# Four PSUM tiles in place of one during the first block of a fused attention and feed-forward kernel

## The chip, the cores and the metric

One Trainium2 chip, one of its cores. The time is the device time of one execution in microseconds (us). Lower is better. TensorE is called PE here, VectorE DVE, ScalarE ACT, GpSimd POOL, and SP is the engine that issues most of the loads and stores.

## What is computed

Three stages follow each other on 2304 rows (4 batches of 576 positions, 512 columns): windowed attention, a gated feed-forward part, and a gated convolution part.

```python
# attention: 8 heads of 64, each position sees itself and 63 before it
scores = scale * q @ k.T                      # masked outside 0 <= i-j < 64
attn = softmax(scores); x = attn @ v          # then heads side by side: (B, 576, 512)
# feed-forward with a mix of each row and the row before it
xk = mu_k*x + (1-mu_k)*x_prev; xr = mu_r*x + (1-mu_r)*x_prev
k = relu(xk @ w_k); v = (k*k) @ w_v; r = sigmoid(xr @ w_r); y = r*v
# five-tap convolution gate
gate = sigmoid(sum_k conv_w[k] * y[t-4+k]); out = (gate * (y @ w_val)) @ w_out
```

## The kernel before

The 2304 rows are cut into five blocks: block 0 has 256 rows, blocks 1 to 4 have 512 each. A **unit** is one block and one pair of heads, so units 0 to 3 are block 0, units 4 to 7 are block 1. For every unit the attention runs through the same steps, and the plan gives each a name:

- `ldqk`, `ldv`: the loads of q, k and v, issued by SP.
- `qk`: the scores, on PE. Units 0 to 3 write them to tiles of the pool `p0` (line 458 to 465), units 4 and up to the first two banks of the shared tile `sv` (line 511).
- `mask` (units 4 and up, DVE, line 518) reads the scores from `sv` and writes the masked ones to SBUF; `edge` on POOL finishes the mask.
- `top`, `exp`, `eps`, `rec`, `norm`: the softmax, on DVE, ACT (line 424), POOL or DVE, and DVE.
- `tp` (units 0 to 3, PE, line 477): transposes of the softmax into the third bank of `sv`; `pt` copies them to SBUF (ACT line 481 or DVE line 482). Later units use a transpose on DVE (`tr`, line 533).
- `pv` (PE, line 488 for units 0 to 3, line 545 later): the values, into the fourth bank of `sv` (all four banks for later units). `x` copies the result to `xT` (ACT line 442 or DVE line 441).

The rest of a block then runs on `xT`: `a` and `xm` mix rows (lines 579 and 592), `r`, `h` and `v` are the three products (line 655 in block 0, line 632 in blocks 1 to 4). PE meets the product `r` first. The weights arrive in pieces: the load `ld`, then `g`, `t`, `s` (lines 348, 351, 353) which convert the words, then `hi` and `lo` (lines 369 to 372) which split each weight in two.

PSUM has eight banks here: `p0` takes four in the first block (two tiles of two banks), `sv` the other four. The pool `pg` takes over the four of `p0` after the last `exp` of block 0 and serves the products.

Nothing is scheduled at run time. Every step is given to a `Plan`, and the table `SLOT` holds a number for each step, by which all of them are sorted; that order is each engine's program order, and a letter (a, v, p) in front of a number says which engine does a step that can run on several. The waits between engines come from the tiles: an instruction that writes a tile waits for the earlier readers of that tile. The four banks of `sv` are one tile, allocated once:

```python
def first_idle():
    Q["sv"] = pq.tile([P, 4, TB], F32, tag="sv", name="sv")
```

`Plan.run` also calls `fill` where its own table of costs sees a gap on PE: it emits matmuls of zeros (line 1197), into `sv` before `pg` exists and into a spare tile of `pg` afterwards, until the first product `r` is emitted.

Of the kernel before, what the change touches and what calls it, by code (L numbers as in the profile page):

```python
# [20 lines left out]
P = 128  # L21
W = 64
# [149 lines left out]
}  # L172

class Plan:

# [1078 lines left out]
```

## Time and profile before

| | us |
|---|---|
| median of three runs | 417.67 (417.37 to 419.25) |
| the profiled execution, its own time | 418.32 |
| span of the profiled execution, first to last instruction | 416.5 |
| PE busy | 405.7 (97% of the span) |
| DVE busy | 341.9 (82%) |
| ACT busy | 256.2 (62%) |
| POOL busy | 28.4 (7%) |

The time of an execution is about 1.8 us longer than its span, which is what lies before the first and after the last instruction. A busy share is an average over stages with different limits: what a change is worth is read in its own stage, from what an engine waited for there. In the rows below, "[1.13 <-DVE s L518]" behind an instruction says that its engine was idle for 1.13 us ahead of it and that the instruction at line 518 on DVE ended the wait. PEclk is the granted clock of PE, 1.00 for 2.4 GHz and 0.50 for 1.2 GHz; a value between says that both levels fell into the stretch.

### The profile page before, as it was taken

The numbers are of one execution on the slowest core, as the hardware profiler recorded it, in microseconds if no ns is written. First come the engines' busy times: TensorE is split into PE (matmuls) and PEld (weight loads), VectorE is DVE, ScalarE is ACT, GpSimd is POOL, SyncE is SP. The second block draws the span as 40 slices with busy tenths as digits, with TensorE's granted clock in tenths as the row PEclk, the third lists the DMA queues.
The fourth block names the chain that finished last, engine by engine and source line by source line (L and its number), as shares of the span: only waits on it lengthen the run. The fifth ranks groups of instructions, "written<-read, shape, count | busy, mean of one in ns | idle before, by whom it ended". The sixth has DMA issues, their size and how long they took to land.

```text
span 416.5 us, 10815 instructions
## 1 busy us (share of the span) xinstructions
PE 405.7 (97%) x4554; PEld 343.0 (82%) x4556; DVE 341.9 (82%) x502; ACT 256.2 (62%) x580; POOL 28.4 (7%) x83
## 2 busy tenths in 40 slices
PE   8599999999999999999999999999999999999996
PEld 4468888878778878777888888888888999999995
DVE  4689899888857848897989898978697899999850
ACT  4769998659553276769424855267631375796741
POOL 3101000001000001000000000000000001023110
PEclk9679999999999999999999999999999999999999
DMA  8976961233113342225443544678999925939945
GB/s 297 412 306 227 330 228 41 68 106 114 59 41 118 137 128 69 82 78 186 134 156 123 211 144 187 214 272 286 347 385 409 368 92 147 248 78 205 218 122 151
DMA packets 26017, 78.36 MB, mean 188 GB/s; under 512 B 2672, under 2 KB 3440, under 8 KB 23920
## 3 DMA queue, kind: packets, MB, share of 16 engines
q1 hardware_dynamic: 23952, 72.64, 48.9%
q0 software_dynamic: 1872, 5.01, 7.2%
q8 instruction: 36, 0.59, 0.6%
q14 instruction: 13, 0.11, 0.1%
q10 hardware_dynamic: 144, 0.00, 0.0%
HBM read 51.80 MB, written 23.49 MB: 181 GB/s over the span
## 4 chain that ended last, share of the span: by engine, by line
PE 95%; ACT 3%; DVE 1%; issue 0%; POOL 0%; DVEq 0%; ACTq 0%; POOLq 0%
PE h L632 21%; PE v L632 21%; PE r L632 11%; PE sv L545 4%; PE h L655 4%; PE v L655 4%; PE sv L511 4%; PE out L1011 3%; PE val1m L901 3%; PE val0m L901 3%; PE val2m L901 3%; PE out2m L901 3%; PE val3m L901 3%; PE out0m L901 3%; PE out1m L901 3%; PE sv L1197 1%
## 5 line engine op out<-in xcount | busy, mean ns | idle before, releaser
L632 PE MATMUL h<-x,wk 128*128 128x512 f32 x384 | 90.5, 393 | 0.0
L632 PEld LDWEIGHTS h<-x,wk 128*128 128x128 f32 x384 | 71.4, 188 | 15.5
L632 PE MATMUL v<-sh,wv 128*128 128x512 f32 x256 | 81.6, 393 | 0.0
L632 PEld LDWEIGHTS v<-sh,wv 128*128 128x128 f32 x256 | 48.0, 188 | 10.8
L424 ACT ACTIVATE s<-s,m 128x96 f32<-128x96 f32 x128 | 46.1, 363 | 12.3 <-DVE m L413 12.2
L632 PE MATMUL v<-sl,wv 128*128 128x512 f32 x128 | 49.9, 390 | 0.0
L632 PE MATMUL r<-x,wr 128*128 128x512 f32 x192 | 45.6, 393 | 0.0
L832 DVE SCALAR_TENSOR_TENSOR early<-early,wc 128x576 f32<-128x576 f32 x48 | 38.4, 813 | 4.7 <-ACT early L830 4.3
L632 PEld LDWEIGHTS r<-x,wr 128*128 128x128 f32 x192 | 35.6, 188 | 7.8
L632 PEld LDWEIGHTS v<-sl,wv 128*128 128x128 f32 x128 | 24.0, 188 | 4.8
L682 ACT ACTIVATE rk<-h 128x512 f32<-128x512 f32 (+1 forms) x27 | 14.2, 536 | 16.7 <-PE h L632 10.8
L424 ACT ACTIVATION_READ_ACCUMULATOR s<-s,m 128x1 f32 x128 | 24.2, 189 | 0.0
L545 PEld LDWEIGHTS sv<-pt,vt 32*64 32x64 f32 x1536 | 18.8, 130 | 5.6 <-issue 2.8
L518 DVE SCALAR_TENSOR_TENSOR s<-sv,band 128x768 f32<-128x768 f32 x16 | 15.3, 955 | 9.2 <-PE sv L511 5.7
L592 DVE SCALAR_TENSOR_TENSOR xm<-xT,omu,xm 128x512 f32<-128x512 f32 x32 | 22.5, 743 | 0.0
L579 ACT ACTIVATE xm<-xT,sm 128x512 f32<-128x512 f32 x26 | 17.0, 712 | 8.0 <-DVE x L615 7.9
L712 DVE TENSOR_TENSOR sl<-rk,sh 128x1024 fp32r<-128x1024 f32 x16 | 19.4, 1220 | 1.5 <-ACT rk L710 1.4
L545 PE MATMUL sv<-pt,vt 32*64 32x32 f32 (+2 forms) x1536 | 20.5, 238 | 0.0
L615 DVE TENSOR_TENSOR x<-xm,x 128x1024 fp32r<-128x1024 f32 x16 | 19.5, 1217 | 0.4 <-ACT x L612 0.4
L511 PEld LDWEIGHTS sv<-qk 64*32 64x32 f32 x1024 | 12.9, 108 | 8.2 <-issue 3.8
L706 ACT ACTIVATE sh<-rk 128x1024 fp32r<-128x1024 f32 x16 | 16.9, 1056 | 3.8 <-DVE rk L684 3.6
L511 PE MATMUL sv<-qk 64*32 64x96 f32 x1024 | 16.5, 255 | 2.7 <-ACT pt L481 1.7
(189 smaller groups left out, 797.4 us busy)
## 6 DMA issues: line engine op xcount, KB each, us to landing
qk<-qk SPq DMA_DIRECT2D x16, 544.0 KB, 4.8
vt<-vh SPq DMA_DIRECT2D x16, 384.0 KB, 3.9
xb<-x2d SPq DMA_DIRECT2D x4, 1152.0 KB, 8.3
out_t<-st SPq DMA_DIRECT2D x15, 288.0 KB, 3.7
x2d<-sgs SPq DMA_DIRECT2D x16, 256.0 KB, 4.0
w_out<-w SPq DMA_DIRECT2D x8, 512.0 KB, 3.0
w_val<-w SPq DMA_DIRECT2D x8, 448.0 KB, 4.2
wk<-w_val SPq DMA_DIRECT2D x2, 1792.0 KB, 11.8
```

The lines of the kernel that those rows point to most:

```text
L424: ACT.activation(out=s, in_=s if t else scores()[:, c // 2, c % 2, :], func=AF.Exp, scale=1.0 if t else D ** -0.5, bias=l(0)[:, c:c + 1], ...
L511: PE.matmul(a["ps"][rows(c), h, j * P:j * P + KW], lhsT=a["q"][heads[h], c * HW:(c + 1) * HW], rhs=a["k"][heads[h], c * HW:c * HW + KW], s ...
L545: PE.matmul(a["o"][heads[h], i, j0 * HW:j1 * HW], lhsT=a["v"][r, k, heads[h]], rhs=p, start=k == 0, stop=k == m + 1, skip_group_check=True)
L579: ACT.activation(out=m[:, i, :n], in_=xT[:, f, 1:1 + n], func=AF.Copy, scale=sm[:, c:c + 1])
L592: V.scalar_tensor_tensor(out=m, in0=xT[:, f, :n], scalar=omu[:, c:c + 1], in1=m, op0=ALU.mult, op1=ALU.add)
L615: lambda E: E.tensor_tensor(out=dst(1), in0=src(), in1=f32(dst(0)), op=ALU.subtract))
L632: PE.matmul(ps, lhsT=a, rhs=b[:, kt, :], start=(kt == 0 and i == 0), stop=(kt == nk - 1 and i == 2))
L655: PE.matmul(Ps[key][:, :n], lhsT=ws(kt), rhs=x()[:, kt, :], start=kt == 0, stop=kt == nk - 1)
L706: ACT.activation(out=Ss[t][0][:, f, :n], in_=rk(), func=AF.Square)
L712: lambda E: E.tensor_tensor(out=Ss[t][1][:, f, :n], in0=rk(), in1=f32(Ss[t][0][:, f, :n]), op=ALU.subtract))
L832: V.scalar_tensor_tensor(out=o, in0=x, scalar=c, in1=o, op0=ALU.mult, op1=ALU.add)
L901: PE.matmul(z[bank][:, j, :HS], lhsT=lhs, rhs=rhs, start=new and kt == 0 and e == 0, stop=kt == 1 and e == 2, skip_group_check=not new)
```

## The change

During the first block the four banks of `sv` are three tiles: `s4` (two banks) for the scores of units 4 and 5, `tp` for the transposes, `pv` for the values. When the values of units 0 to 3 have been copied out and the scores of units 4 and 5 have been masked, the pool is closed and one tile `sv` of four banks takes its place for the rest of the kernel. Matmuls of zeros ahead of `pg` go to the first bank of `s4` until unit 4 has its scores, then to `pv` if `tp` holds something that was not yet read, else to `tp`, and to none if both hold something.

```diff
-    pq = pas.enter_context(tc.tile_pool(name="pq", bufs=1, space=PSUM, side="right"))
+    pzs = ExitStack()
+    pz = pzs.enter_context(tc.tile_pool(name="pz", bufs=1, space=PSUM, side="right"))
...
         def tp():
+            held.add("tp")
...
-                PE.transpose(Q["sv"][:, 2, i * P:(i + 1) * P], a["s"][:, i, :], ident)
+                PE.transpose(Q["tp"][:, i * P:(i + 1) * P], a["s"][:, i, :], ident)
...
         def pv():
-            a["o"] = Q["sv"]
+            held.add("pv")
+            a["o"] = Q["pv"]
...
+        early_scores = u < HP + 2
...
-            a["ps"] = Q["sv"]
+            a["ps"] = Q["s4"] if early_scores else Q["sv"]
...
     def first_idle():
-        Q["sv"] = pq.tile([P, 4, TB], F32, tag="sv", name="sv")
+        Q["s4"] = pz.tile([P, 2, TB], F32, tag="s4", name="s4")
+        Q["tp"], Q["pv"] = (pz.tile([P, TB], F32, tag=n, name=n) for n in ("tp", "pv"))
     op("idle", "none", 0, ["warm"], first_idle)
+
+    def strips_space():
+        pzs.close()
+        Q["sv"] = pas.enter_context(tc.tile_pool(name="pq", bufs=1, space=PSUM, side="right")).tile([P, 4, TB], F32, tag="sv", name="sv")
+    op("sv", "none", 0, [*[("x", u) for u in range(HP)], *[("mask", HP + i) for i in range(2)]], strips_space)
...
-        elif any("ps" in A[u] for u in range(HP, len(UNITS))):
+        elif "ps" not in A[HP]:
+            ps = Q["s4"][:, 0]
+        elif len(held) < 2:
+            ps = Q["pv" if "tp" in held else "tp"]
+        else:
             return
-        else:
-            ps = Q["sv"][:, 0]
```

The table `SLOT` is new from one end to the other, so the order on every engine is another, over the whole kernel. Two of its lines:

```diff
-    'qk': '9 11 19 34 38 57 109 142 177 246 261 304 341 367 387 431 467 497 519 546',
+    'qk': '9 12 19 34 26 57 99 145 180 242 262 312 341 362 398 416 444 493 521 555',
-    'pt': 'a33 a51 v70 a87',
+    'pt': 'a36 a59 a71 a86',
```

Steps that may run on ACT or DVE change sides as well. In all, DVE gains 15 of them (six splits `xhi`, two squares `sq`, two splits of `w_out`, two `ghi`, one `xhi_`, one `ghi_`, one split of `w_k`) and gives up two (`pt` of unit 2 and one split of `w_val`) and two small `eps`. The counts of products and of attention matmuls stay; the matmuls of zeros grow from 24 to 28.

**PE, from the scores of unit 3 on.** Before; `qk_227` and `qk_262` are the inputs of units 4 and 5, `pt` the transposed softmax, `spare` the tile in `pg`:

```order
L465 MATMUL qk_245<-early 64x128 x8
L511 MATMUL sv<-qk_227 32x96 x32
L488 MATMUL sv<-pt_238,sgs 64x64 x8
L477 MATMUL sv<-ident,xm 128x128 x4
L511 MATMUL sv<-qk_262 32x96 x32
L488 MATMUL sv<-pt_316,sgs 64x64 x8
L1197 MATMUL spare<-sgs 128x512
```

Scores, values and transposes alternate, and all of them write `sv`.

The same place in the changed kernel, from the scores of unit 2 on (`qk_190` and `qk_295` are the inputs of units 4 and 5, `s_122` is the tile `s4`):

```order
L467 MATMUL qk_206<-early 64x128 x8
L521 MATMUL s_122<-qk_190 32x96 x32
L480 MATMUL tp<-ident,xm 128x128 x4
...
L467 MATMUL qk_278<-early 64x128 x8
L1215 MATMUL tp<-sgs 128x512
...
L494 MATMUL pv<-pt_266,sgs 64x64 x8
...
L1215 MATMUL pv<-sgs 128x512
L521 MATMUL s_122<-qk_295 32x96 x32
L494 MATMUL pv<-pt_323,sgs 64x64 x8
```

The scores of unit 4 stand ahead of the transposes of unit 0 now; four matmuls of zeros into `tp` stand ahead of the values of unit 0, and one into `pv` behind the transposes of unit 1.

**SP, the first loads.** Before (`early` holds q and k of units 0 to 3, `sgs` and `rk` their v, `x` and `s` the first two weight pieces):

```order
L397 DMA early<-qk 128x576 x4
L403 DMA sgs<-vh 128x512
L397 DMA qk_227<-qk 128x1088
L366 DMA x_118<-w_r 128x2048
L397 DMA qk_262<-qk 128x1088
L403 DMA rk<-vh 128x512
L403 DMA sgs<-vh 128x512
L366 DMA s_119<-w_r 128x2048
```

Unit 4's q and k come sixth, behind the v of unit 0, and the second piece of `w_r` comes eleventh, behind the v of units 2 and 1.

In the changed kernel:

```order
L399 DMA early<-qk 128x576 x3
L399 DMA qk_190<-qk 128x1088
L399 DMA early<-qk 128x576
L368 DMA x_119<-w_r 128x2048
L405 DMA sgs<-vh 128x512 x2
L399 DMA qk_295<-qk 128x1088
L368 DMA s_120<-w_r 128x2048
L405 DMA rk<-vh 128x512 x2
```

Unit 4's q and k move to fourth place, and the v of units 2 and 3 behind the second piece of `w_r`.

**ACT, from the softmax of unit 2 on.** Before (`xm` holds the exponentials of block 0, `s_298` those of unit 4):

```order
L424 ACTIVATE xm,first_m<-qk_205,first_m 128x128 x4
L481 ACTIVATE pt_238<-sv 128x512
L424 ACTIVATE xm,first_m<-qk_245,first_m 128x128 x4
L348 ACTIVATE words<-x_118 128x1024
L481 ACTIVATE pt_316<-sv 128x512
L442 ACTIVATE xT<-sv 128x256
L424 ACTIVATE s_298,m_323<-s_298,m_323 128x96 x8
L579 ACTIVATE x_118<-xT,sm 128x256 x2
L348 ACTIVATE words<-s_119 128x1024
```

The copy `pt` of unit 2 is on DVE, that of unit 3 comes later than these rows.

In the changed kernel:

```order
L426 ACTIVATE xm,first_m<-qk_206,first_m 128x128 x4
L486 ACTIVATE pt_266<-tp 128x512
L350 ACTIVATE words<-x_119 128x1024
L426 ACTIVATE xm,first_m<-qk_278,first_m 128x128 x4
L486 ACTIVATE pt_323<-tp 128x512
L426 ACTIVATE s_298,m_333<-s_298,m_333 128x96 x8
L444 ACTIVATE xT<-pv 128x256
L486 ACTIVATE pt_400<-tp 128x512
L589 ACTIVATE x_119<-xT,sm 128x256 x2
L350 ACTIVATE words<-s_120 128x1024
L486 ACTIVATE pt_429<-tp 128x512
```

All four copies `pt` are on ACT, each in turn behind one piece of softmax or weight work, and the copy `x` of unit 0 has left for DVE.

## Rows read from the trace of the kernel before

**Rows 1.** All waits of PE over the span: for whom, us, times, longest.
```profile
PE sv L511 <- ACT pt L481: 1.7, 1, 1.7
PE sv L488 <- DVE s L518: 1.1, 1, 1.1
PE sv L477 <- DVE s L518: 1.1, 1, 1.1
...
PE sv L511 <- ACT xT L442: 1.0, 1, 1.0
...
PE h L655 <- ACT sgs L722: 0.2, 1, 0.2
```

**Rows 2.** Timeline of PE: start us, us, instructions, idle before and its end.
```profile
6.60 1.68 PE L1197 MATMUL sv<-sgs 128*128 128x512 bf16 x7 [0.27 <-issue]
...
9.02 0.63 PE L477 MATMUL sv<-ident,xm 128*128 128x128 f32 x4
...
14.24 1.12 PE L488 MATMUL sv<-pt,sgs 128*64 128x64 f32 x16 [1.13 <-DVE s L518]
15.30 1.12 PE L477 MATMUL sv<-ident,xm 128*128 128x128 f32 x4
17.38 1.53 PE L511 MATMUL sv<-qk 64*32 64x96 f32 x64 [0.96 <-ACT xT L442]
...
22.85 1.91 PE L1197 MATMUL spare<-sgs 128*128 128x512 bf16 x4 [0.22 <-issue]
...
27.97 0.69 PE L488 MATMUL sv<-pt,rk 128*64 128x64 f32 x16
28.58 2.86 PE L655 MATMUL r<-x,words 128*128 128x256 f32 x12
31.37 1.00 PE L511 MATMUL sv<-qk 64*32 64x96 f32 x64
```

**Rows 3.** Stretches: us, busy of PE, PEld, DVE, ACT, POOL, then PEclk, DMA, GB/s.
```profile
10.00:12.00 2.00, 0.38 (x14) 0.13 (x6) 1.51 (x4) 1.93 (x10) 0.00 (x0) 1.00 0.99 401
12.00:14.00 2.00, 1.00 (x64) 0.78 (x64) 0.77 (x1) 2.00 (x10) 0.00 (x0) 0.84 1.07 424
14.00:16.00 2.00, 1.76 (x20) 1.64 (x20) 1.74 (x4) 0.47 (x1) 1.10 (x4) 0.50 0.98 401
26.00:28.00 2.00, 1.96 (x10) 1.03 (x9) 2.00 (x4) 0.93 (x3) 0.00 (x0) 0.75 0.99 407
10.00:28.00 18.00, 12.78 (x213) 8.37 (x206) 12.86 (x24) 11.43 (x43) 2.07 (x7) 0.62 1.02 414
```

**Rows 4.** The chain of waits: start us, us, ACT's pieces in and behind the first block.
```profile
10.07 1.50 ACT xm L424 x8
...
16.45 0.60 ACT pt L481
17.05 0.28 ACT xT L442
...
27.91 1.04 ACT words L348
...
30.17 0.79 ACT x L579 x2
30.96 2.87 ACT s L424 x16
```

**Rows 5.** SP's timeline of the two loads that move, at issue.
```profile
3.06 0.43 SPq L397 DMA_DIRECT2D qk<-qk  x1
...
5.90 0.44 SPq L366 DMA_DIRECT2D s<-w_r  x1
```

**Rows 6.** The same two loads in the DMA view: KB, us from issue to landing.
```profile
qk<-qk SPq DMA_DIRECT2D x1, 544.0 KB, 5.9
...
s<-w_r SPq DMA_DIRECT2D x1, 1024.0 KB, 12.0
```

**Rows 7.** DVE at its fullest: a stretch of the last part, columns as above.
```profile
360.00:380.00 20.00, 20.00 (x152) 20.00 (x151) 20.00 (x29) 15.56 (x26) 3.24 (x4) 1.00 0.68 152
```

**Rows 8.** Timeline of DVE: one split of 1024 columns, as the change moves.
```profile
209.55 0.69 DVE L613 CAST x<-xm 128x1024 fp32r<-128x1024 f32 x1
```

More of the change, by code (lines that the diff above doesn't have):

```diff
@@ L293, in tile_kernel @@
     p0 = p0s.enter_context(tc.tile_pool(name="p0", bufs=2, space=PSUM))
-    pq = pas.enter_context(tc.tile_pool(name="pq", bufs=1, space=PSUM, side="right"))
-    plan = Plan(p0=2, pg=4, sv=1, pa=1, pb=1, valu=1, valv=1, outu=1, outv=1)
+    pzs = ExitStack()
+    pz = pzs.enter_context(tc.tile_pool(name="pz", bufs=1, space=PSUM, side="right"))
+    plan = Plan(p0=2, pg=4, sv=1, s4=1, pa=1, pb=1, valu=1, valv=1, outu=1, outv=1)
     op = plan.op
@@ L372, in weight @@
            lambda E: E.tensor_tensor(out=dst[1], in0=s(), in1=f32(dst[0]), op=ALU.subtract))
-    A = {}
+    A, held = {}, set()
     UNITS = [(t, hp) for t in range(NB) for hp in range(HP)]
@@ L474, in tp, with src @@
         def tp():
+            held.add("tp")
             a["pt"] = mx.tile([P, 8 * KW + HW], F32, tag="pt", name=f"pt{u}")[:, :2 * n].rearrange("p (h q) -> p h q", h=2)
             for i in range(2 * n2):
-                PE.transpose(Q["sv"][:, 2, i * P:(i + 1) * P], a["s"][:, i, :], ident)
+                PE.transpose(Q["tp"][:, i * P:(i + 1) * P], a["s"][:, i, :], ident)
         op(("tp", u), "pe", 480, [("norm", u), "ident", *([("pv", u - 1)] if u else [])], tp, ring=("pa", ("pt", u)))
-        src = lambda: Q["sv"][:, 2].rearrange("p (h q) -> p h q", h=2)
+        def src():
+            held.discard("tp")
+            return Q["tp"].rearrange("p (h q) -> p h q", h=2)
         plan.any(("pt", u), [("tp", u)],
@@ L484, in pv, with o @@
         def pv():
-            a["o"] = Q["sv"]
+            held.add("pv")
+            a["o"] = Q["pv"]
             for c in range(nc_):
                 for h in range(2):
-                    PE.matmul(a["o"][heads[h], 3, c * W:(c + 1) * W], lhsT=a["v"][:, c, heads[h]],
+                    PE.matmul(a["o"][heads[h], c * W:(c + 1) * W], lhsT=a["v"][:, c, heads[h]],
                               rhs=a["pt"][:, h, c * W:(c + 1) * W], start=True, stop=True)
         op(("pv", u), "pe", 615, [("pt", u), ("ldv", u)], pv, ring=("pb", ("x", u)))
-        place_x(u, 0, u, lambda: a["o"][:, 3, :n].rearrange("p (i c) -> p i c", c=W), W)
+        def o():
+            held.discard("pv")
+            return a["o"][:, :n].rearrange("p (i c) -> p i c", c=W)
+        place_x(u, 0, u, o, W)
     def unit(u):
@@ L512, in qk @@
                                   rhs=a["k"][heads[h], c * HW:c * HW + KW], start=True, stop=True)
-        op(("qk", u), "pe", 1160, [("ldqk", u)], qk, ring=("sv", ("mask", u)))
+        op(("qk", u), "pe", 1160, [("ldqk", u), "idle" if early_scores else "sv"], qk, ring=("s4" if early_scores else "sv", ("mask", u)))
         def mask():
@@ L546, in pv @@
                                   start=k == 0, stop=k == m + 1, skip_group_check=True)
-        op(("pv", u), "pe", 1210, [("tr", u), ("ldv", u), *([("x", w) for w in range(HP)] if t == 1 else [])], pv, ring=("sv", ("x", u)))
+        op(("pv", u), "pe", 1210, [("tr", u), ("ldv", u), "sv"], pv, ring=("sv", ("x", u)))
         place_x(u, t, hp, lambda: a["o"][:, :, :P], P)
```

251 rows, old and new, of the table SLOT are left out of this document.

## The prediction, on record before the changed kernel was run

> **What bounds the kernel now.** I read the list of all waits of PE first. Outside the first microseconds and a wait of 0.2 us, PE waits four times, and all four are on the tile `sv` [rows 1]: 1.7 us for ACT's copy `pt`, 1.1 us twice for DVE's `mask`, 1.0 us for ACT's copy `x`, 4.9 us together. After these the list is empty, so from the first product `r` at 28.58 us [rows 2] PE runs through to the last store. What reaches the end is therefore the time at which `r` can start; all work behind it is the same set of matmuls in either kernel.
>
> The timeline of PE [rows 2] shows what the four waits are. The scores of unit 5 wait for a copy out of the fourth bank, which they don't touch; the values of unit 0 wait for `mask`, which reads banks one and two, while they write bank four. Each writer waits for readers of other banks, because the four banks are one tile.
>
> The table of stretches [rows 3] shows a second cost. In 10 to 12 us PE is busy for 0.38 us, in 12 to 14 us for 1.00 us, and the granted clock drops: 0.84 over 12 to 14 us is full clock until about 13.4 us, then 0.50, and 0.75 over 26 to 28 us is a return at about 27.0 us. At the low level the same pieces take longer [rows 2]: values 1.12 us against 0.69, transposes 1.12 against 0.63, scores of a later unit 1.53 against 1.00, a matmul of zeros 0.48 (1.91 / 4) against 0.24 (1.68 / 7).
>
> **The change part by part.** I follow the new order from the softmax of unit 2, which I leave where it is: ACT begins it at 10.07 us [rows 4], and nothing ahead of it is moved on PE, DVE or ACT.
>
> *Scores of unit 4.* Their load landed at 3.06 + 5.9 = 9.0 us, the second piece of `w_r` at 5.90 + 12.0 = 17.9 us [rows 5, 6]. Between the two, 3104 KB came in (sizes by the shapes in the order rows: 1024 + 544 + 256 + 256 + 1024), 349 KB a microsecond. The load moves ahead of 256 and 288 KB, so 544 / 349 = 1.6 us earlier, to 7.4 us: no wait. The 1.00 us of scores [rows 2] falls into what was PE's wait of 1.7 us [rows 1] and costs nothing; 0.7 us of the gap remains. The load of unit 3's scores, now one place later, is used only after these.
>
> *Values of unit 0, transposes of unit 1.* `pt` of unit 0 ends at 10.07 + 1.50 + 0.60 = 12.2 us [rows 4]. The four matmuls of zeros ahead of the values write `tp`, so they wait for that same read and don't fill the gap: they cost 4 x 0.24 = 0.96 us. Values to 13.8 us, transposes of unit 1 to 14.5 us, with 0.69 and 0.63 us [rows 2]. Before, these transposes ended at 15.30 + 1.12 = 16.4 us. The v load of unit 0 now has the first `w_r` piece ahead of it; up to its end 1024 KB more come in than came up to 9.0 us before, so it lands at 9.0 + 1024 / 349 = 11.9 us, in time.
>
> *Unit 5 and unit 1's values.* On ACT follow the word conversion of `w_r` (1.04), the softmax of unit 3 (1.50) and `pt` of unit 1 (0.60) [rows 4]: 15.3 us. PE meanwhile has one matmul of zeros, which waits for DVE's copy of unit 0, the scores of unit 5, then the values of unit 1 and the transposes of unit 2: 14.5 + 0.24 + 1.00 + 0.69 + 0.63 = 17.0 us.
>
> *Unit 2.* ACT: the softmax of unit 4 (2.87), `x` of unit 1 (0.28), `pt` of unit 2 (0.60), 19.1 us [rows 4]. PE's six matmuls of zeros (1.4 us) end at 18.5 us, beside it. The v of unit 2 is now where the second `w_r` piece was, at 17.9 us. Values and transposes of unit 3 to 19.1 + 0.69 + 0.63 = 20.4 us.
>
> *Unit 3.* ACT: `a` (0.79), the conversion of the second `w_r` piece (1.04; it lands 256 KB earlier, at 17.2 us) and `pt` (0.60), 21.5 us [rows 4]. Three matmuls of zeros end beside it. Values 0.69: `r` starts at 22.2 us, against 28.58: **6.4 us earlier**.
>
> *What is late next.* ACT sets the last two steps, the v load of unit 2 is 1.2 us ahead of them, and DVE is close: it was busy 12.86 us between 10 and 28 us [rows 3]. If its new list ahead of `r`'s first input were as long and had no idle, that input would come at 22.9 us, a gain of 5.7 us. The new list leaves out `pt` of unit 2 and has pieces of unit 4 later, but `lo` of the first weight piece earlier, so I take ACT's 22.2 us. At the other end, were ACT's pieces no limit, the v load at 17.9 us would still be followed by 0.69, 0.63, a `pt` of 0.60 and 0.69 us, 20.5 us, a gain of 8.1 us; that needs the weight conversion of unit 3's turn to vanish, so I keep only part of it.
>
> *Behind `r`.* The one new tile `sv` waits for the copies of unit 3 before unit 6 writes it; in the old order the same scores come after the first `r` products too, and in the new one two `r` parts (about 1.9 us by 2.86 / 3 each [rows 2]) stand ahead, longer than `x` of unit 3 (0.28). DVE takes 15 more pieces from ACT and gives up two of like size; at 0.69 us for the common one [rows 8] that is some 9 us. I cost them at nothing on the path, because PE never waited for DVE after the first block [rows 1]; without that cover they are the slower rival below.
>
> The sum: the profiled execution took 418.32 us, less 6.4 is 411.9. It stands 0.65 us above the median of 417.67, so the forecast against the median is **411.3 us**, if the clock stays up.
>
> Does it? Before, the drop followed two stretches with PE busy 0.38 of 2 and 1.00 of 2 us [rows 3]. In the new order the longest idle time by the steps above is about 0.7 us (11.5 to 12.2), then 0.1, then 0.6 and 0.4 ahead of the values of units 2 and 3. I take it that the clock stays at 2.4 GHz. The Trainium skill (TensorE: Matmul & The Clock Gate, Part 1: The HAM clock gate) speaks against building on this: it says that the count of cold matmuls varies from run to run, that the ramp costs under 1% of a typical span, and that a model should not be fitted to it. By that page alone one would leave the clock's part out and forecast what the first rival gives.
>
> **The rivals.**
>
> *The clock falls as before.* The cold prices of [rows 2] from 13.4 us on: values of unit 0 to 13.8, then transposes 1.12, zeros 0.48, scores 1.53, values 1.12, transposes 1.12 (19.2 us), six zeros 2.9, values and transposes 2.2, three zeros 1.4, values 1.12: `r` at 26.8 us. Here the matmuls of zeros, ten on the path, cost more than they hide. Gain 1.8 us, 415.9 us. For it: at 14 to 16 us PE was busy 1.76 of 2 and the clock stayed low [rows 3], so once down it does not come back quickly. Against it: the gap that preceded the drop is filled. If the clock is low for half of that time the gain is about 4.1 us, 413.6 us.
>
> *The release does not reach `r`.* DVE, ACT and POOL pass the softmax round between them, and each piece there is queued behind others on two engines. If DVE's list ahead of `r`'s input is longer than I think, or its waits for POOL and ACT add 4 to 6 us of idle, `r` starts at 27 to 28.6 us and the time is 416 to 417.7 us. For it: DVE idled 5.1 of these 18 us [rows 3]. Against it: part of this idle was waiting for PE, through the tile.
>
> *Slower: DVE becomes PE's bound in the later blocks.* The 13 net pieces, 9.0 us, all on the path against the lead of 6.4 give 420.3 us. For it: DVE is busy 20.00 of 20 us at 360 to 380 us [rows 7]. Against it: only about three of these pieces belong to that part, and DVE is idle for 18% of the span. It decides from 8.5 us of PE's waits for DVE on (6.4 and the 2.1 below).
>
> *The change doesn't do what it says.* That the zeros fill the gap is already not so for the first four; the tiles themselves are split as the order rows show, so this is in the sum and has no case of its own.
>
> **How the numbers follow.** About 0.5% (2.1 us) is what a measurement of this kernel can tell from no change. The forecast 0.55; low clock for part of the time 0.17 (413.6); low as before 0.10 (415.9, just inside 2.1 us, so I share it between faster and same); lead not reaching `r` 0.10 (same); slower 0.08. Faster: 0.55 + 0.17 + 0.06 = 0.78; same 0.14; slower 0.08. The range reaches from 409.8 (7.9 us gained: near the end set by the v load) to 415.9, the cold case, which leaves out the last two rivals, 0.18.
>
> **What would show it.** Right: no wait of PE on scores or values for a reader of another bank; scores of unit 4 before 10.5 us; PEclk at 1.00 from 8 to 28 us; `r` at 21.5 to 23 us, and the end earlier by the same amount. Wrong: PEclk 0.50 in any stretch there; a wait of PE for DVE or ACT behind `r` of more than 1 us; `r` held by `xm` rather than by the values of unit 3.

## The result, and the profile after

The changed kernel takes 413.22 us (median of four runs, 412.41 to 415.29) against 417.61 us for the kernel before beside it: 0.989 of the time, interval 0.985 to 0.994. The forecast was 411.3 us with a range of 409.8 to 415.9. In a second comparison the changed kernel took 412.77 us (after_again, below). Ratios, their intervals and the table by clock further down leave out the slow executions, those more than 1.5% above the fastest of the same kernel.

The profiled execution of the changed kernel is its slowest one, 415.29 us with a span of 413.5 us, so its profile shows 3.0 us less than that of before (418.32) where the medians show 4.4.

| | before | after |
|---|---|---|
| span, us | 416.5 | 413.5 |
| PE busy | 405.7 | 403.5 |
| DVE busy | 341.9 | 351.5 |
| ACT busy | 256.2 | 243.1 |
| mean granted clock of PE | 0.983 | 0.994 |

The list of PE's waits after (for whom, us in total, times, longest):

```profile
PE val0m L911 <- ACT early L923: 1.8, 1, 1.8
PE s L1215 <- POOL sgs L306: 1.1, 1, 1.1
PE s L521 <- DMA qk<-qk: 1.0, 1, 1.0
PE tp L1215 <- ACT pt L486: 1.0, 1, 1.0
PE sv L521 <- ACT xT L444: 0.5, 1, 0.5
```

None of the four waits of [rows 1] for a reader of another bank is left. What stands now in the first block is a wait for a load (1.0 us) and one of the zeros for `pt`, the copy out of the very bank that they write (1.0 us); the one for POOL is in the first microseconds, as before. The 0.5 us are the scores of unit 6, the first to write the new tile `sv` of four banks, which is there only when the copy `x` of unit 3 is done. The longest, 1.8 us, is of a kind that the old list does not have: it lies behind `r`, in the last part of the program.

PE's timeline of the first block:

```profile
11.82 1.02 PE L1215 MATMUL tp<-sgs 128*128 128x512 bf16 x3 [0.95 <-ACT pt L486]
12.77 0.69 PE L494 MATMUL pv<-pt,sgs 128*64 128x64 f32 x16
13.39 0.66 PE L480 MATMUL tp<-ident,xm 128*128 128x128 f32 x4
...
15.32 1.00 PE L521 MATMUL s<-qk 64*32 64x96 f32 x64 [0.97 <-DMA qk<-qk]
...
20.79 0.69 PE L494 MATMUL pv<-pt,rk 128*64 128x64 f32 x16
21.40 2.00 PE L665 MATMUL r<-x,words 128*128 128x256 f32 x8
23.88 0.36 PE L521 MATMUL sv<-qk 64*32 64x96 f32 x10 [0.48 <-ACT xT L444]
```

The last row is cut off by the end of the view. `r` starts at 21.40 us; before it was 28.58 [rows 2], so 7.2 us were gained there (in a second traced execution of the old kernel, before_look, it was 26.90 us). The values take 0.69 us, not 1.12.

The table of stretches (us, busy of PE, PEld, DVE, ACT, POOL, then PEclk, DMA share, GB/s), for the stretches of [rows 3, 7] and for the stretch with the new wait:

```profile
10.00:12.00 2.00, 1.04 (x25) 0.74 (x24) 1.97 (x5) 2.00 (x10) 0.48 (x3) 1.00 1.00 397
12.00:14.00 2.00, 1.95 (x24) 1.22 (x23) 2.00 (x6) 2.00 (x8) 0.00 (x0) 1.00 1.08 440
14.00:16.00 2.00, 1.03 (x61) 0.68 (x64) 1.84 (x3) 2.00 (x10) 1.25 (x1) 1.00 0.96 389
10.00:28.00 18.00, 15.37 (x263) 11.07 (x264) 16.71 (x29) 16.32 (x62) 3.24 (x7) 1.00 1.02 416
324.00:326.00 2.00, 0.20 (x2) 0.00 (x0) 1.69 (x3) 1.73 (x3) 0.00 (x0) 1.00 1.04 380
326.00:328.00 2.00, 1.97 (x10) 1.98 (x11) 2.00 (x3) 1.66 (x3) 0.00 (x0) 0.63 1.03 404
328.00:330.00 2.00, 2.00 (x10) 2.00 (x10) 1.50 (x3) 0.68 (x1) 0.00 (x0) 0.52 0.93 359
360.00:380.00 20.00, 20.00 (x152) 20.00 (x151) 19.88 (x29) 17.55 (x28) 4.34 (x5) 1.00 0.66 138
```

Over 10 to 28 us the clock is 1.00 where it was 0.62. At 324 to 326 us PE is idle for 1.8 of 2 us, and the clock then stands at 0.63 and 0.52 for two stretches: a new fall, late in the program, in this execution.

Where did the 7.2 us go? The first `val0m`, the product that opens the last part, cuts the span in three: up to `r`, from `r` to `val0m`, and from there to the end. These are the starts in PE's timeline of the profiled execution of each kernel that will be used (the lower ones are experiments):

| kernel | `r` at | `r` to `val0m` | `val0m` to the end |
|---|---|---|---|
| before | 28.58 | 292.1 | 95.8 |
| before, once more (before_look) | 26.90 | 292.5 | 95.5 |
| after | 21.40 | 293.1 | 99.1 |
| after, once more (after_again) | 21.49 | 293.8 | 97.3 |
| old order, split tiles (split_only) | 22.61 | 292.1 | 97.9 |
| old order, one tile, clock held (hold_clock) | 24.38 | 292.0 | 97.1 |
| early load of `w_out` (wo2_early) | 21.88 | 291.9 | 95.5 |
| the same, once more (wo2_again) | 21.12 | 293.5 | 95.5 |

In the profile of after 1.0 us is given back between `r` and `val0m` and 3.3 us behind `val0m`. Of the 1.0 us, 0.48 are the wait of the scores of unit 6; the rest stays unexplained, and the two executions of one kernel in the last two rows differ there by 1.6 us. ACT's timeline shows the second place (start us, us, instruction, idle before and its end):

```profile
320.07 0.64 ACT L923 ACTIVATE early<-val0m 128x576 f32<-128x576 f32 x1
324.27 1.16 ACT L806 ACTIVATE x<-xb 128x1152 fp32r<-128x1152 f32 x1 [3.57 <-DMA xb<-x2d]
325.34 0.63 ACT L923 ACTIVATE early<-val0m 128x576 f32<-128x576 f32 x1
```

And PE's timeline there:

```profile
326.03 4.97 PE L911 MATMUL val0m<-x,wk 128*128 128x288 f32 x24 [1.82 <-ACT early L923]
```

ACT waits for the load of `xb` (it landed 9.6 us after its issue at 314.64), and the copy of `val0m` that PE needs stands behind it. Then the 24 matmuls take 4.97 us; in the kernel before, PE came to the same 24 without a wait, and they took 3.51 us at full clock:

```profile
330.27 3.51 PE L901 MATMUL val0m<-x,wk 128*128 128x288 f32 x24
```

The wait of 1.82 us and the low clock, 4.97 - 3.51 = 1.46 us, are the 3.3 us. This is the slowest execution of its four: in after_again the same wait was 1.1 us, the clock stayed at 1.00, and from `val0m` to the end it took 97.3 us.

SP's timeline shows what stands ahead of this load in the changed order:

```profile
298.11 0.43 SPq L1174 DMA_DIRECT2D wr<-w_out  x1
310.43 0.37 SPq L848 DMA_DIRECT2D gd<-early  x1
310.85 0.46 SPq L1174 DMA_DIRECT2D wr<-w_out  x1
314.64 0.53 SPq L774 DMA_DIRECT2D xb<-x2d  x1
```

The second piece of `w_out` (1024 KB) stands behind a store that cannot go before 310.43 us, and comes in just ahead of `xb`. In the kernel before both pieces of `w_out` were issued together at 299.65 us.

### The profile page after: what moved, and what is told of

Read it like the earlier page. It is cut to its first block, busy times and chain, and to the rows that moved or that the text cites. A ratio compares the mean times of both kernels' runs of the same rounds, so it can differ in the third digit from the quotient of the medians.

```text
span 413.5 us, 10816 instructions
## 1 busy us (share of the span) xinstructions
PE 403.5 (98%) x4557; PEld 342.3 (83%) x4560; DVE 351.5 (85%) x513; ACT 243.1 (59%) x567; POOL 30.5 (7%) x85
## 4 chain that ended last, share of the span: by engine, by line
PE 86%; DMA 9%; DVE 2%; issue 1%; SPq 0%; ACT 0%; POOL 0%; ACTq 0%
PE v L642 22%; PE h L642 21%; PE r L642 11%; PE sv L555 5%; PE v L665 4%; DMA words<-w_k 3%; PE out L1021 3%; PE out1m L911 3%; PE out2m L911 3%; PE val1m L911 3%; PE val3m L911 3%; PE val2m L911 3%; PE sv L521 3%; DMA xb<-x2d 2%; PE out0m L911 2%; DMA early<-qk 2%
## 5 line engine op out<-in xcount | busy, mean ns | idle before, releaser
L555 PE MATMUL sv<-pt,vt 32*64 32x64 f32 (+2 forms) x1536 | 21.1, 237 | 0.2
L840 ACT ACTIVATE early<-early,wc 128x576 f32<-128x576 f32 x12 | 9.0, 774 | 20.4 <-DMA gd<-early 14.1
L528 DVE SCALAR_TENSOR_TENSOR s<-sv,band 128x768 f32<-128x768 f32 x14 | 13.3, 954 | 4.8 <-PE sv L521 4.4
L732 ACT ACTIVATE sgs<-r 128x512 f32<-128x512 f32 (+1 forms) x20 | 10.5, 550 | 10.9 <-PE r L642 10.9
```

The source lines that it names most:

```text
L555: PE.matmul(a["o"][heads[h], i, j0 * HW:j1 * HW], lhsT=a["v"][r, k, heads[h]], rhs=p, start=k == 0, stop=k == m + 1, skip_group_check=True)
```

## The experiments

Two questions: which part of the change gave the lead at `r` (the split tile, the clock, the new order), and what took part of it back. Eleven runs were made, two of them of kernels already seen (after_again, before_look) and one a repetition (wo2_again), each compared in five rounds with the kernel before on its chip. A ratio is to that kernel.

**one_tile.** The new order with the four banks in one tile again.

```diff
-        Q["s4"] = pz.tile([P, 2, TB], F32, tag="s4", name="s4")
-        Q["tp"], Q["pv"] = (pz.tile([P, TB], F32, tag=n, name=n) for n in ("tp", "pv"))
+        first = pz.tile([P, 4, TB], F32, tag="first", name="first")
+        Q["s4"], Q["tp"], Q["pv"] = first[:, :2], first[:, 2], first[:, 3]
```

> The new order with its matmuls of zeros, but s4, tp and pv are parts of one tile of four banks again, so every writer waits for readers of other banks. If the split of the tile is what matters: waits of PE for mask, pt and x of other banks come back, about 3 us of them between 13 and 24 us; r starts at 24.8 us if the clock stays up and at 28.7 us if it falls, against 21.4 us with the split, and the time is 3 to 7 us above the changed kernel's, 416 to 420 us. If the new order alone brings the gain: r within 1 us of 21.4 us and the time within 1 us of the changed kernel's 413.2 us.

Measured: 422.11 us, ratio 1.011 (1.005 to 1.016). PE's waits:

```profile
PE first L480 <- DVE s L528: 3.4, 1, 3.4
PE first L1215 <- DVE s L528: 2.0, 1, 2.0
PE first L1215 <- DVE xT L443: 1.0, 1, 1.0
PE first L494 <- ACT pt L486: 0.7, 1, 0.7
PE first L480 <- DVE xT L443: 0.6, 1, 0.6
```

The waits for readers of another bank are back: 3.4, 2.0 and 0.6 us, 6.0 together. The wait for `pt` is for an input, and the 1.0 us is a matmul of zeros that writes the bank of the values and waits for the copy `x` of unit 0 out of that same bank. `r` starts at 28.98 us, and the time lies above the expected 416 to 420 us. The new order alone is slower than the old kernel: it is only usable with the split.

**split_only.** The table `SLOT` of before with the split tiles and the new step `sv`; of the changed rule for zeros only the part that uses `s4` until unit 4 has its scores.

```diff
-        Q["sv"] = pq.tile([P, 4, TB], F32, tag="sv", name="sv")
+        Q["s4"] = pz.tile([P, 2, TB], F32, tag="s4", name="s4")
+        Q["tp"], Q["pv"] = (pz.tile([P, TB], F32, tag=n, name=n) for n in ("tp", "pv"))
```

> The old order with the tile split and no matmuls of zeros into tp or pv. If the split is what matters: scores of unit 5 and values of unit 0 no longer wait, r starts at 21.7 us with the clock up and at 24.9 us if it falls at 13.4 us as before; the time is 3.5 to 7 us below before, 410.5 to 414 us. If the new order is needed (its zeros hold the clock): the clock falls in 10 to 27 us and the gain is 3.7 us or less. If the split alone does nothing: r at 28 us, 417 to 418 us.

Measured: 413.21 us, ratio 0.989 (0.984 to 0.994); `r` at 22.61 us. By the times the split in the old order gives as much as the whole change, and the new order adds nothing that shows. The scores of unit 5 waited all the same, in their middle, and the profile names nothing that ended this wait:

```profile
15.27 0.57 PE L521 MATMUL s<-qk 64*32 64x96 f32 x32 [1.68 <-issue]
```

Then the clock fell for a time: 0.50 over 16 to 18 us. The wait of `val0m` for ACT is there too (1.7 us, after which the clock stayed at 1.00), although the old table issues both pieces of `w_out` together. SP's timeline, then ACT's:

```profile
293.65 2.04 SPq L1174 DMA_DIRECT2D wr<-w_out  x2
314.88 0.54 SPq L774 DMA_DIRECT2D xb<-x2d  x1
```

```profile
324.38 1.17 ACT L806 ACTIVATE x<-xb 128x1152 fp32r<-128x1152 f32 x1 [3.99 <-DMA xb<-x2d]
```

`xb` landed 9.5 us after its issue, against 7.5 us in the kernel before. So the late piece of `w_out` is not needed for this wait: a kernel that comes to this load 6 us earlier finds it slow in the old order as well. In one_tile, which has the new table and no lead, `xb` took 8.8 us and `val0m` waited 1.0 us. Either one, the lead or the new place of the load, goes with a later `xb`.

**no_bridge.** The changed kernel without the five matmuls of zeros into `tp` and `pv`.

```diff
-        elif len(held) < 2:
-            ps = Q["pv" if "tp" in held else "tp"]
```

> The changed kernel without the five matmuls of zeros into tp and pv. By the forecast these five do not fill the gap ahead of the values of unit 0 but follow it: without them the values of unit 0 start 0.9 us earlier, r is unchanged if the clock stays up (ACT sets the last two steps), and the time is that of the changed kernel within 1 us. If they hold the clock: PEclk falls below 1.00 between 10 and 17 us, r starts at about 25 us, and the time is 3 to 4 us above the changed kernel's.

Measured: 414.88 us, ratio 0.993 (0.990 to 0.997). Stretches:

```profile
14.00:16.00 2.00, 0.63 (x54) 0.63 (x60) 1.91 (x4) 2.00 (x12) 1.31 (x1) 1.00 0.98 398
16.00:18.00 2.00, 2.00 (x52) 1.68 (x36) 1.77 (x4) 2.00 (x12) 0.11 (x1) 0.66 1.03 419
18.00:20.00 2.00, 2.00 (x6) 0.74 (x5) 2.00 (x3) 1.79 (x5) 1.34 (x3) 0.50 1.06 424
```

The values of unit 0 come 0.7 us earlier (12.06 against 12.77 us), as without zeros in front they must; yet `r` comes at 23.05 us, 1.65 us later than in after. The scores of unit 5 wait for their load until about the same time in both (15.37 and 15.32 us), so without the zeros PE idles longer ahead of these scores, 2.03 us against 0.97:

```profile
15.37 0.99 PE L521 MATMUL s<-qk 64*32 64x96 f32 x64 [2.03 <-DMA qk<-qk]
```

PE was busy for 0.63 us of 14 to 16, and the clock fell behind it. So the zeros, which wait for the same copy as the values and fill no gap ahead of it, shorten the gap that follows. The trace shows the fall; the times lie between the two expectations, and their interval overlaps that of the changed kernel (0.988 to 0.994 in after_again), so its price is not shown. Nor does every such gap end in a fall: in after_again these scores waited 1.4 us, PE was busy for 0.65 us of 14 to 16, and the clock stayed at 1.00.

**before_look.** This and the next one ask how much of the old time was the clock. Every execution comes with PE's mean granted clock.

> The old kernel itself with a profile of every execution's mean clock beside the time. Clock theory: the time falls with the mean clock, and executions at 0.998 or more lie at 413 to 415 us, those at 0.985 or less at 417 to 419 us. Waits theory: the time does not follow the clock.

Measured: 418.70 us, and its profiled execution (416.71 us, mean clock 0.986) has the four waits of [rows 1] (1.5, 1.1, 1.1 and 1.0 us). Of its own executions those at 0.997 and more took 414.4 to 414.7 us, those at 0.985 and less 418.2 to 420.3. The table has 71 executions of the kernel before from these comparisons:

| mean granted clock | executions | us, median (lowest to highest) |
|---|---|---|
| 0.998 to 1.000 | 13 | 414.4 (413.0 to 415.5) |
| between | 31 | 416.8 (414.4 to 419.5) |
| 0.985 and less | 27 | 418.6 (417.1 to 420.3) |

The same program, with the same order of work, is 4.2 us apart by the clock. This goes together; whether the clock is the cause, the next run tests.

**hold_clock.** The old order, and scores, transposes and values in one tile still (in three banks). The fourth bank is only for matmuls of zeros, those of `fill` among them, which wait for nothing.

```diff
-        Q["sv"] = pq.tile([P, 4, TB], F32, tag="sv", name="sv")
+        first = pz.tile([P, 3, TB], F32, tag="first", name="first")
+        Q["s4"], Q["tp"], Q["pv"] = first, first[:, 2], first[:, :2].rearrange("p h (c j) -> p (h c) j", j=P)[:, :, KW:]
+        Q["zz"] = pz.tile([P, TB], F32, tag="zz", name="zz")
...
+            if u == 0:
+                zeros(4)
...
+            if early_scores:
+                zeros(7 if u == HP else 3)
```

> The old order, the scores, transposes and values of the first block still in one tile (three banks; the values lie in the columns that the scores leave free), so that every wait on the shared tile stays. The fourth bank is a tile for matmuls of zeros alone, which wait for nothing: 7 of them ahead of the scores of unit 4, 4 ahead of the values of unit 0, 3 ahead of the scores of unit 5, each lot as long as the wait that it stands in or shorter (1.7, 1.1 and 1.0 us). Clock theory (most of the gain is that PE's clock stays up, since the executions of the old kernel with a mean clock of 0.998 or more took 413.0 to 414.8 us): PEclk 1.00 from 8 to 28 us, r at 24 to 25 us against 28.58, waits on the tile first of 2 us or more still there, 413 to 414.5 us, and few executions above 415. Waits theory (the gain is the 4.9 us of waits on the shared tile): r stays behind 26 us and the time within 1 us of the old kernel, 416 to 418 us, whatever the clock does.

Measured: 413.90 us (413.42 to 415.32, twelve executions, each at a mean clock of 0.998 or more), ratio 0.994 (0.990 to 0.997). PE's timeline:

```profile
10.31 1.68 PE L441 MATMUL zz<-sgs 128*128 128x512 bf16 x7
12.05 1.00 PE L530 MATMUL first<-qk 64*32 64x96 f32 x64
12.98 1.04 PE L441 MATMUL zz<-sgs 128*128 128x512 bf16 x4
14.18 0.69 PE L501 MATMUL first<-pt,sgs 128*64 128x64 f32 x16 [0.16 <-DVE s L537]
14.79 0.65 PE L485 MATMUL first<-ident,xm 128*128 128x128 f32 x4
...
24.38 2.86 PE L674 MATMUL r<-x,words 128*128 128x256 f32 x12
```

The reader can lay this beside [rows 2]. The values of unit 0 start at 14.18 us, before at 14.24: the shared tile holds PE up as long as it did. But the gaps are full of zeros, the clock is 1.00 in every stretch to 30 us, and the pieces behind take 0.69 and 0.65 us where they took 1.12. `r` starts 4.2 us earlier, and by the ratio the time is 2.6 us (1.3 to 4.0) below the kernel before. What was expected of listed waits was wrong: 1.7 us of waits on `first` are listed, not 2 or more, because zeros now stand in them. The cause is shown: this part of the old kernel's time was the clock, and it is regained without taking one wait away. By the same measure the changed kernel gains 4.4 us (ratio 0.989) or 3.8 us (0.991), so the clock is more than half of it, as far as overlapping intervals tell.

**after_again, evict_first, x3_first, both** ran together. after_again is the changed kernel.

> The changed kernel itself, to stand beside the three edits below on one chip. Expected 0.988 to 0.991 of the kernel before, some 413 us; in the profile r at 21.4 us and a wait of about 1.8 us of val0m for ACT's copy at line 923, behind a load of xb that lands over 9 us after its issue. If the wait at val0m belongs to single executions and not to the order of the work, it is missing here.

Measured: 412.77 us, ratio 0.991 (0.988 to 0.994), the wait of `val0m` 1.1 us. It is not of one execution, then; its length varies, and this time the clock did not fall behind it.

evict_first exchanges ACT's copy of `val0m` and its split of `xb`:

```diff
-    'xhi_': 'v859 a875 v848 v857 v885 v889 a911 a929 a915 a914 a955 a937 a965 a973 a984 a995 a1002 a1016 a1075 '
+    'xhi_': 'v859 a875 v848 v857 v885 v889 a912 a929 a915 a914 a955 a937 a965 a973 a984 a995 a1002 a1016 a1075 '
...
-    'valu': 'v898 a909 a912 a931 a949 a954 a1003 a1022 a1040 a1095 a1121 a1137',
+    'valu': 'v898 a909 a911 a931 a949 a954 a1003 a1022 a1040 a1095 a1121 a1137',
```

> The changed kernel with two instructions of ACT exchanged: the copy of the second val0m (line 923) goes ahead of the split of xb (line 806, which waits for the load of xb). Theory (ACT's copy stands in a queue behind a load that is late): val0m's wait of 1.8 us for ACT falls to 0.7 us or less, what remains being for DVE's split of xb, since the second dozen of its matmuls needs xb; the clock stays at 1.00 over 324 to 332 us, where matmuls ran at both levels; together 1.1 to 2.5 us less, 411 to 412 us. Rival (the load of xb itself is what val0m needs, the copy only happens to stand last): a wait of about 1.8 us remains there, put down to DVE or ACT's piece of xb, and the time stays at 413 us.

Measured: 413.15 us, ratio 0.993 (0.990 to 0.997): no gain on after_again that the times show, so the forecast of 411 to 412 us was missed. The list of waits says why the exchange is worth little:

```profile
PE val0m L911 <- DVE early L952: 0.7, 1, 0.7
```

The wait moved to DVE, where a sum that reads `val0m` stands behind another split of `xb`. Two engines' queues are held up by the same load.

wo2_early (which ran first, with one_tile) instead issues the second piece of `w_out` ahead of the store that held it:

```diff
-    'wo2': '904 887 883 843',
+    'wo2': '886 887 883 843',
```

> The changed kernel with one store-back load of w_out (1024 KB) issued ahead of the last gate store on SP instead of behind it. In the changed kernel SP stands at that store until 310.4 us, the load goes out at 310.9 us and the load xb at 314.6 us lands 9.6 us later; PE waits 1.8 us for a copy queued on ACT behind xb, and the clock falls there in the profiled run. If the place of this load is the cause: xb lands about 2.5 us sooner, PE's wait of 1.8 us is gone, and the time is 1.5 to 3 us below the changed kernel's, 410.2 to 411.7 us. If the DMA engines are simply full there whatever the order: the wait stays above 1 us and the time is within 0.5 us of 413.2 us.

Measured: 411.13 us, ratio 0.985 (0.980 to 0.990). SP's and PE's timelines:

```profile
297.43 1.01 SPq L1174 DMA_DIRECT2D wr<-w_out  x2
309.63 0.37 SPq L848 DMA_DIRECT2D gd<-early  x1
313.97 0.53 SPq L774 DMA_DIRECT2D xb<-x2d  x1
```

```profile
323.39 3.36 PE L911 MATMUL val0m<-x,wk 128*128 128x288 f32 x24
```

`xb` landed 6.9 us after its issue instead of 9.6; PE comes to the 24 matmuls without a wait, they run at full clock, and `val0m` to the end takes 95.5 us, as in the kernel before (95.8). It was run again on another chip:

> The changed kernel with the early load of w_out once more, to see whether 411.1 us holds on another chip or day: theory (the wait at val0m comes from a late load of xb) 411 us with no wait of val0m for ACT; rival (it was scatter) 412.5 to 413 us, like the changed kernel.

Measured: 411.43 us, ratio 0.989 (0.984 to 0.993), again 95.5 us behind `val0m` and no wait there.

x3_first puts the copy of unit 3 ahead of a word conversion on ACT, to take away the 0.5 us ahead of the scores of unit 6:

```diff
-    'w_k g': '88 121 128 160',
+    'w_k g': '90 121 128 160',
```

> The changed kernel with the copy x of unit 3 ahead of the word conversion of w_k on ACT, which waits 1.7 us for its load. Theory (waits of PE in the lead reach the end one to one): the wait of 0.5 us ahead of the scores of unit 6 goes, and 0.5 us of the time with it if the later wait at val0m does not take it, which is too little to tell from the changed kernel by the times; the place to see it is the start of the last block's h, 0.5 us earlier. Rival (a lead gained early is taken by the load of xb at 314 us): h starts earlier but val0m waits 0.5 us longer, same end.

Measured: 412.93 us, ratio 0.993 (0.989 to 0.996). The scores of unit 6 follow `r` at 23.50 us with no wait, but so they do in after_again without the edit, at 23.41 us (its wait of 0.8 us for a load is at 45.05 us, at the scores of a later unit). The 0.5 us were of one execution. Inconclusive: there was nothing to take away, and 0.5 us is below what five rounds tell.

both joins it with the early load.

> The early load of w_out and the copy x of unit 3 ahead of the conversion together. Theory (two separate waits of PE, each reaching the end): no wait of val0m, no wait of 0.5 us at the scores of unit 6, and 410.6 us, 0.5 below the early load alone (411.1). Rival (the wait of 0.5 us hid others): 411.1 or more.

Measured: 411.40 us, ratio 0.990 (0.985 to 0.995): nothing beyond the early load, as the rival had it. The three runs with the early load have medians of 411.1, 411.4 and 411.4 us over 17 executions, the changed kernel 413.2 and 412.8. On the chip where they stood side by side (both and after_again) that is 1.4 us, and their intervals overlap; the order of the medians, the vanished wait and the 95.5 us agree in all three.

## Why the prediction was right

*The four waits on `sv`.* As forecast, all are gone; one_tile brings such waits back, 6.0 us in the new order, and there `r` is 7.6 us later than with the split.

*The start of `r`.* Forecast 22.2 us, measured 21.40. ACT began unit 2's softmax at 9.78 us, 0.3 earlier than before (10.07 [rows 4]); that nothing ahead of it was moved is not so, a small DVE piece (`omu`) now ends ACT's wait there. Its copies `pt` ended a little ahead of the forecast each time: unit 0's at 11.76 against 12.2. The order of events was as forecast, with ACT and PE close together.

*The zeros fill nothing.* Right for the wait: PE was idle for 0.95 us ahead of the four zeros, for the same `pt`. The 0.96 us were counted as pure cost, though; in the trace of no_bridge `r` comes 1.65 us later without them.

*The load of unit 5.* Not in the working. It moved behind the v of units 0 and 1, and the scores of unit 5 waited 0.97 us for it. This delayed nothing, since ACT set the steps behind: it had no idle time from 9.78 to 20.74 us.

*The clock.* The forecast said 1.00 from 8 to 28 us, and it was, in spite of two idle stretches of about 1 us instead of 0.7. Its price was in the numbers, though never drawn out: the forecast gained 6.4 us with the clock up and its cold rival 1.8, so the clock was worth 4.6. The runs show 2.6 us by the ratio of hold_clock (4.2 us at `r` in its trace) and 4.2 by the clocks of the old kernel's executions. With the clock up on both sides 1.6 us are left: the changed kernel's 14 executions at 0.998 or more (the first comparison and after_again) have a median of 412.8 us, the old kernel's 13, partly on other chips, one of 414.4. The first paragraph of the prediction put the four waits in front; in the old order they are, by these runs, the smaller part, and what they did above all was to leave PE idle, after which the clock fell. The split tile and the new order together bring `r` from 24.38 us (hold_clock) to 21.40, 3.0 us more; of these the medians show about 1 us (413.9 to 412.8 and 413.2), and 2.5 to 2.8 us once the load of `w_out` is early.

The Trainium skill (TensorE: Matmul & The Clock Gate, Part 1: The HAM clock gate) holds that the count of cold matmuls varies from run to run and that the ramp is under 1% of a typical span. It says both of the ramp at a kernel's start. These 71 executions vary as well, with mean clocks of 0.981 to 1.000; a fall of the clock in mid-program, of which that sentence does not speak, goes here with 4.2 of 418.6 us, 1.0%, and by hold_clock with more than half of the gain.

*Behind `r`.* The step that failed. "I cost them at nothing on the path, because PE never waited for DVE after the first block": I looked at DVE's pieces and not at the loads of the last part. DVE was nearly no bound, as that sentence has it (no wait for it in the profile of after, 0.9 us at most in after_again). But the load of `xb` was, through ACT: 1.8 us of wait and 1.5 us of low clock in the profile of after, 1.1 us of wait in after_again. A wait of more than 1 us for ACT behind `r` was named as a sign of a wrong forecast. By the traces two things go with a later landing of that load, and the sum has neither: the new place of the `w_out` load (one_tile, and wo2_early, which undoes it) and the lead itself (split_only). The scores of unit 6, also put at nothing, waited 0.5 us for `x` of unit 3 in one of the two traces.

With the one load moved back, the two runs gave 411.1 and 411.4 us, close to the forecast of 411.3. In part that is luck: `r` came 0.3 and 1.1 us earlier than forecast in their traces, and in the second 1.4 us went again between `r` and `val0m`, which no run explains. That 413.2 us lies in the range is luck too, since its upper end was set by the cold rival and not by a loss behind `r`.

*The slower rival* did not come: DVE is as busy at 360 to 380 us as before (19.88 against 20.00 [rows 7]). *The lead not reaching `r`* did not come either. *The cold rival* did not come; the kernel without bridging zeros shows a shorter fall (414.9 us, `r` at 23.05 us).

What stays open: how the changed kernel's lead of 1.2 us at `r` over split_only is lost (one execution of each was traced, and the medians differ by less than either's spread), where the time between `r` and `val0m` goes in some executions, and why the lead alone makes the load of `xb` slower (9.5 us in split_only against 7.5), when both kernels keep the DMA engines full there (a share of 0.9 to 1.06 around 320 to 330 us).

## What to carry to other kernels

When a wait is followed by a granted clock of 0.50, price the two apart: the wait by its length, the clock by the slow pieces behind it. Matmuls of zeros in a bank of their own gave back 2.6 us here (4.2 us at `r`) with every wait left in place. When a whole order is replaced, go through the loads of the far end as well: a lead of 7 us at the start met one load there that lands late, and a queue on two engines behind it; issuing another load earlier took that wait away.

## What was not expected

The time of one and the same program follows PE's mean granted clock, 414.4 us at 0.998 and more, 418.6 us at 0.985 and less. That the clock does not fall in every execution after the same waits is the likely reason, but no execution of the old kernel at a high clock was traced. With the gaps filled the spread shrinks: twelve executions of hold_clock lie within 1.9 us, sixteen of the kernel before, beside it on the same chip, within 5.9 us (413.23 to 419.08).

In one_tile PE was busy for 0.69 us at 18 to 20 us and not at all at 20 to 22, and the clock was still 1.00 in both stretches:

```profile
18.00:20.00 2.00, 0.69 (x16) 0.55 (x16) 0.00 (x0) 2.00 (x12) 0.00 (x0) 1.00 0.98 405
20.00:22.00 2.00, 0.00 (x0) 0.00 (x0) 0.78 (x1) 1.19 (x7) 0.20 (x1) 1.00 1.04 420
22.00:24.00 2.00, 1.77 (x7) 1.04 (x8) 2.00 (x5) 0.88 (x2) 0.28 (x2) 0.64 1.00 413
24.00:26.00 2.00, 2.00 (x12) 0.73 (x12) 1.12 (x1) 1.54 (x3) 0.00 (x0) 0.51 1.00 418
```

It fell behind the gap, at 22 to 26 us, when PE was at work again: here the price of an idle stretch was paid by the pieces after it.
